# A Fourier mixing layer and a mixture of experts: stage four in even and odd products on quarters of the array

## The chip, the cores and the metric

The kernel runs on one core of one Trainium2 chip. The metric is the device time of one execution in microseconds, as the median of several runs. A core has TensorE (matrix products out of SBUF into PSUM, which has eight banks of 2 KB per partition), VectorE, ScalarE and GpSimd (called DVE, ACT and POOL in the profile), and SyncE (SP), which here issues most of the transfers. Each engine works through its own list of instructions in order and waits on semaphores where one needs another's result.

## What is computed

The first half multiplies each batch of 2496 tokens by 256 features with a filter in the frequency domain, along the tokens. The second sends each token to the one of 8 experts with the largest logit, applies two matrix products with a ReLU between them, and scales by the gate.

```python
# 8 batches, S = 2496, D = 256; all fp32
X = np.fft.rfft(x, axis=1)
y = np.fft.irfft(X * (filt_r + 1j * filt_i)[None], n=S, axis=1)
x = y.reshape(19968, 256)
logits = x @ w_gate                      # (256, 8)
e = np.argmax(logits, axis=1)
gate = softmax(logits)[range(N), e]
out[t] = gate[t] * (np.maximum(x[t] @ w1[e], 0) @ w2[e])   # w1 (8,256,1024), w2 (8,1024,256)
```

## The kernel before

The transform of length 2496 is split as 39 times 64 (the two have no common factor, so tokens and frequencies are only renumbered, and nothing is multiplied in between). A real transform of length 39 has 20 frequencies, each with a real and an imaginary part. So a batch goes through four stages, each a product with a fixed table: stage one (`stage_a`, table `ta`) takes 39 tokens to 20 complex frequencies, stage two (`stage_b`, `tb`) does the complex transform of length 64 and multiplies by the filter, stage three (`stage_c`, `tc`) goes back over the 64, and stage four (`stage_d`, table `td`, tile `tds`) takes 20 complex frequencies back to 39 real tokens. Three groups of 39 tokens stand side by side, so stage four multiplies 3 x 40 = 120 rows onto 3 x 39 = 117 outputs (padded to 128). A batch has 22 such columns of 256 features (the last has only one group, 40 rows). They come in chunks of four, `CH`: five of four columns and one of two. A product takes two columns, which fill one bank of 512 fp32. So a chunk of four is two products, each followed by a copy out of the bank into `yo` (`evac`, which picks VectorE or ScalarE by which the planner thinks is free first). In a chunk of two each column has a product of its own, of 120 and of 40 rows.

Between stages one and two and between three and four the data go through DRAM (`zd`, `ud`), since the partition axis changes: `stage_c` stores four frequencies of all 64 x 2 rows with one transfer of 4 KB runs per partition (`by_part`), and `load_u` reads whole columns of 120 rows (`columns`) into `fin`. Batch 0 is turned on the chip instead (`first_a`, `turn_z`, `first_c`, `turn_u`).

After stage four, `turn_y` transposes `yo` in blocks of 32 on VectorE (from batch 3 on), `block_logits` multiplies by the gate weights on four column quarters of the array (tile `lt`), `block_back` turns the logits back, and `route` finds expert, gate and the row of each token in a list by expert, writes token number and gate behind its features in `yo`, and scatters each column with one indirect transfer of GpSimd into `rows`. `tile_map` and `rows_in` then take tiles of 512, 256 or 128 rows of one expert from there. `first_products` and `second_products` are the two streams of the experts' products. Tiles of 512 rows use seven quarter products in place of eight (`hidden_by_quarters`, and after the last batch also `result_by_quarters`, the sums of whose weights are made on GpSimd into `tsum`); the plain way is `hidden` and `result`.

The order of the work is written out by a planner in the kernel itself. `Order` keeps a clock for each engine and an estimate for each instruction. `slot(k)` lists the steps of stage two and three of batch k, stage one of batch k + 1 and stage four of batch k - 1, each with a place between 0 and 1, what must be loaded, its TensorE time, a category (steps of one category stay in order) and what it needs. The main loop takes, each time, the first step or expert product whose needs are met by the planned clocks, `share()` of expert time for each unit of transform time. PSUM has seven banks for products; `bank()` takes the one that comes free first by the plan. `more_loads` issues loads ahead into seven `fin` tiles, `flush` sends stores when their data are due. All transfers but scatters are on SP's queue, in the order in which the planner wrote them. Every instruction is issued through one helper, line 246, so the profile's rows are told apart by the tiles' names and not by lines.

Of the kernel before, what the change touches and what calls it, by code (L numbers as in the profile page):

```python
# [19 lines left out]
P = 128  # L20
# [14 lines left out]
TK = NB * NS  # L35
DH = D // P
# [4 lines left out]
NJ = D // CT  # L41

# [13 lines left out]
def dft_tables():  # L56

    w = 2.0 * np.pi
    q = np.arange(N1)
    t = np.arange(N2)

    ta = np.zeros((NB, N1, NB, NS))
    td = np.zeros((NB, NS, NB, N1))
    for f in range(NF):
        ang = w * ((q * f) % N1) / N1
        for j in range(NB):  # L70
            ta[j, :, j, f] = np.cos(ang)
            td[j, f, j] = (2.0 if f else 1.0) / S * np.cos(ang)
            if f:
                ta[j, :, j, NF + f] = -np.sin(ang)
                td[j, NF + f, j] = -2.0 / S * np.sin(ang)

    ang = w * ((t[:, None] * t[None, :]) % N2) / N2
    c, sn = np.cos(ang), np.sin(ang)
    tb = np.block([[c, -sn], [sn, c]]).reshape(2, N2, P).transpose(1, 0, 2).reshape(P, P)
    tc = np.block([[c, sn], [-sn, c]]).reshape(P, 2, N2).transpose(0, 2, 1).reshape(P, P)  # L80

    ids = np.zeros((NB, N1, NG))
    valid = np.zeros((NB, N1, NG))
    for j in range(NB):
        for i in range(len(range(j, N2, NB))):
            ids[j, :, i] = token(q, NB * i + j)
            valid[j, :, i] = 1.0

    by_block = np.zeros((4, CT, NG + 2))
    by_block.reshape(P, NG + 2)[:TP, :NG] = valid.reshape(TP, NG)  # L90
    by_block = by_block.reshape(4, CT, -1, 4).transpose(3, 1, 2, 0).reshape(P, -1)

    sg = np.where(coefficients() <= S // 2, 1.0, -1.0)

    return {
        "ta": ta.reshape(TP, TK),
        "tb": tb,
        "tc": tc,
        "td": np.pad(td.reshape(TK, TP), ((0, 0), (0, P - TP))),
        "sg": np.concatenate([sg[:, :NF // 2], sg[:, NF // 2:]]),  # L100
        "ids": ids.reshape(TP, NG),
        "valid": np.concatenate([np.pad(valid.reshape(TP, NG), ((0, P - TP), (0, 0))), by_block], axis=1),
    }


def lay_x(x):

    out = np.zeros((x.shape[0], P, NG, D), x.dtype)
    q = np.arange(N1)
    for j in range(NB):  # L110
        for i in range(len(range(j, N2, NB))):
            out[:, j * N1:(j + 1) * N1, i] = x[:, token(q, NB * i + j)]
    return out
# [11 lines left out]
class Order:  # L125
# [53 lines left out]
    def count(self, engine, op, args, named):  # L179
# [21 lines left out]
        if op.endswith("dma_start"):  # L201
            busy = 1.03 if engine == "gpsimd" else 0.4
            if engine == "sync":
                start = max(start, self.lands[-8])
            self.t[engine] = start + busy
            took = self.transfer(out, named["in_"])
            self.t["transfers"] = max(self.t["transfers"], start + busy) + took
            end, tail = self.t["transfers"], self.LOAD
            if engine == "sync":
                self.lands = self.lands[-7:] + [end + tail]  # L210
        else:
            if out is None:
                took = 0.8 if engine == "sync" else 0.02
            elif engine == "tensor":
                if start > self.busy + 1.2:
                    self.slow = start + 3.4
                rows = out.ap[0][1]
                took = max(0.1, 0.00085 * n) if op == "transpose" else max(0.216, 0.00169 * n) if rows > 32 else 0.00045 * n
                took *= 2.0 if start < self.slow else 1.0
                tail = 0.25  # L220
            elif engine == "vector":
                took = 0.15 + n / 960
            elif engine == "scalar":
                took = 0.16 + n / 1200
            else:
                took = 0.2 + n / 480
            end = self.t[engine] = start + took
            if engine == "tensor":
                self.busy = end
# [21 lines left out]
class Slots:  # L251
# [3 lines left out]
    def freed(self, name, tag):  # L255
# [3 lines left out]
        if tag in self.live and name in self.live[tag]():  # L259
            return 1e9  # L260
# [33 lines left out]
def kernel(  # L294
# [12 lines left out]
    ids: bass.AP,  # L307
    valid: bass.AP,
# [25 lines left out]
    TR = E * TE  # L334

    dram = open_pool(ctx, name="dram", bufs=1, space=DRAM)
    zd = [dram.tile([N2, NS, D], F32, tag=f"z{b % 2}", name="zd") for b in range(B)]
    ud = [dram.tile([N2, NS, D], F32, tag=f"u{b % 2}", name="ud") for b in range(B)]
# [3 lines left out]
    rowsd = dram.tile([TR, DR], F32, tag="rows", name="rows")  # L342
# [17 lines left out]

    tas = cst.tile([TP, TK], F32, name="tas")
    tbs = cst.tile([P, P], F32, name="tbs")
    tcs = cst.tile([P, P], F32, name="tcs")
    tds = cst.tile([TK, P], F32, name="tds")
# [15 lines left out]
    ids0 = cst.tile([TP, NG], F32, name="ids0")  # L380
    vld = cst.tile([P, 2 * NG + 2], F32, name="vld")
# [12 lines left out]
    ps.live["bank"] = lambda: ()  # L394
# [25 lines left out]
    def load_filters(c):  # L420
        f0, n = FH[c]
        if c == 0:
            nc.sync.dma_start(out=tbs, in_=tb)
            nc.sync.dma_start(out=sgs, in_=sg)
# [10 lines left out]
        if c == 0:  # L435
            nc.sync.dma_start(out=tcs, in_=tcm)

    def load_rest():
        nc.sync.dma_start(out=tds, in_=td)
# [33 lines left out]
    def columns(ap, i0, n):  # L473

        rows = ap.rearrange("t s d -> (t s) d")
        m = min(n, NG - 1 - i0)
        yield TK, slice(0, m), rows[i0 * TK:(i0 + m) * TK, :].rearrange("(i p) d -> p i d", p=TK)
        if m < n:
            yield NS, slice(m, n), rows[(NG - 1) * TK:, :].rearrange("(i p) d -> p i d", p=NS)
# [23 lines left out]
    def by_part(ap):  # L503

        return ap.rearrange("t (c f) d -> (t c) f d", c=2)

# [8 lines left out]
    def load_z(b, c):  # L515
        f0, n = FH[c]
        zi = fin(("z", b, c))
        nc.sync.dma_start(out=zi[:, :n], in_=by_part(zd[b])[:, f0:f0 + n, :])

    def load_u(b, c):  # L520
        i0, n = CH[c]
        ui = fin(("u", b, c))
        for r, m, v in columns(ud[b], i0, n):
# [5 lines left out]

    def stage_a(b, c):  # L530
        i0, n = CH[c]
        xt = ins.pop(("x", b, c))
        zo = sb.tile([TK, 4, D], F32, tag="st", name="zo", bufs=4)
        for j in range(0, n, 2):
            p = bank()
            mm(p[:TK, :], lhsT=tas, rhs=xt[:TP, j:j + 2, :], start=True, stop=True)
            evac(zo[:, j:j + 2, :], p[:TK, :].rearrange("p (t d) -> p t d", t=2), 512)
        for r, m, v in columns(zd[b], i0, n):
# [4 lines left out]
    def stage_b(b, f):  # L543
# [6 lines left out]
        mm(p, lhsT=tbs, rhs=zi[:, j:j + 2, :], start=True, stop=True)  # L550
# [14 lines left out]
    def stage_c(b, f):  # L565
# [4 lines left out]
        uo = outs["u", b]  # L570
        p = bank()
        mm(p, lhsT=tcs, rhs=ys, start=True, stop=True)
        evac(uo[:, j:j + 2, :], p.rearrange("p (i d) -> p i d", i=2), 512)
        if j == 2:
            f0 = f - 2
            move(by_part(ud[b])[:, f0:f0 + 4, :], uo)
# [3 lines left out]
    def stage_d(b, c):  # L580
# [7 lines left out]
        yo = outs["o", b, c] = sb.tile([P, 4, DR], F32, tag="y", name="yo", bufs=YB)  # L588
        for j in range(0, n, 2):
            p = bank()  # L590
            if i0 + j + 2 < NG:
                mm(p, lhsT=tds, rhs=ui[:TK, j:j + 2, :], start=True, stop=True)
# [6 lines left out]


# [12 lines left out]
    def first_a(c):  # L613
        i0, n = CH[c]
        xt = ins.pop(("x", 0, c))
        for j in range(0, n, 2):
            p = bank()[:, :4 * TK]
            for h in range(DH):
                for i in range(2):
                    mm(p[:, (2 * h + i) * TK:(2 * h + i + 1) * TK], lhsT=xt[:TP, j + i, h * P:(h + 1) * P], rhs=tas,  # L620
# [21 lines left out]
    def first_c(f):  # L642
        ys = outs.pop(("y", 0, f))
        p = bank().rearrange("p (h i t c) -> p h i t c", h=DH, c=2, i=2)
        for i in range(2):
            for h in range(DH):
                mm(p[:, h, i].rearrange("p t c -> p (t c)"), lhsT=ys[:, i, h * P:(h + 1) * P],
                   rhs=tcs, start=True, stop=True)
# [90 lines left out]
    def route(b, c0, c1):  # L739
# [63 lines left out]
        if by_blocks(b):  # L803
# [13 lines left out]
            nc.vector.tensor_copy(row.rearrange("p (c g) -> p g c", g=4), pr[:, :, 0])  # L817
# [5 lines left out]
        for i, yo in enumerate(yos):  # L823
            n = min(4, w - 4 * i)
            sh8 = (TP, n, 8)
            nc.gpsimd.tensor_scalar(
                yo.bitcast(I32)[:TP, :n, D:D + 8], in0=ids0[:, t0 + 4 * i:t0 + 4 * i + n, None].to_broadcast(sh8),
# [3 lines left out]
        for i in range(w):  # L831
            m = N1 if t0 + i == NG - 1 else TP
# [116 lines left out]
    def rows_in(i):  # L949
# [4 lines left out]
        ng = gis[i] = pools["moe"].tile([P, 4, DR - D], F32, tag="ng", name="ng", bufs=8)  # L954
# [262 lines left out]
    def slot(k):  # L1217
# [12 lines left out]
        elif k < B:  # L1230
            for f in range(0, NF + 4, 2):
                at = f / (NF + 4)
                if f < NF:
                    steps.append((at, lambda f=f: stage_b(k, f), ("z", k, f // 4) if f % 4 == 0 else None, 0.85, "b", lambda f=f: count("y") < 4 and [ins["z", k, f // 4]]))
                if f >= 4:
                    steps.append((at + 0.01, lambda f=f: stage_c(k, f - 4), None, 0.85, "c", lambda f=f: [outs["y", k, f - 4], 0.0 if f % 4 else sb.free("st") - 0.9]))
        if k + 1 < B:
            for c in range(nch):
                steps.append(((0.25 if k == 0 else 0.0) + 0.7 * c / nch, lambda c=c: stage_a(k + 1, c), ("x", k + 1, c), 0.43 * CH[c][1], "a", lambda c=c: [ins["x", k + 1, c], sb.free("st") - 0.9]))
        if k > 0:  # L1240
            for c in range(nch + 3):
# [3 lines left out]
                if c < nch:  # L1245
                    steps.append((at, lambda c=c: stage_d(k - 1, c), ("u", k - 1, c) if k > 1 else "y", 0.43 * CH[c][1], "d",
                                  lambda c=c: [ins["u", k - 1, c] if k > 1 else outs["ui", c], sb.free("y") - 0.9]))
                if by_blocks(k - 1):
                    if 1 <= c <= nch:
                        steps.append((at + 0.03, lambda c=c: turn_y(k - 1, c - 1), None, 0.0, "d", lambda c=c: len(yts) < 2 and [outs["o", k - 1, c - 1]]))  # L1250
# [174 lines left out]
    def second_products():  # L1425

        for i in range(NT - RARE):
            if late and i < LARGE:
# [37 lines left out]
    with tc.manual_schedule(engines=None):  # L1466
        warm()
        nc.sync.dma_start(out=tas, in_=ta)
# [5 lines left out]
        def wait_of(f):  # L1474
# [11 lines left out]
            banks = ps.free("bank") if f[3] < 0.9 else max(ps.free("bank"), ps.free("bank", 1) - 0.85)  # L1486
# [15 lines left out]
        while fs or any(heads):  # L1502
# [7 lines left out]
            choice[0 if credit > 0.0 or not fs else 1:0] = products  # L1510
# [64 lines left out]
```

## Time and profile before

| | |
|---|---|
| median of 5 runs | 1477.38 us (1475.93 to 1479.08) |
| the profiled execution | 1477.88 us, of which its span 1476.2 us |
| mean granted clock of TensorE | 0.994 |
| TensorE busy | 1440.2 us, 98% of the span |
| VectorE, ScalarE, GpSimd busy | 848.1, 480.7, 821.5 us |
| stage four's products (`bank<-fin,tds`, batches 1 to 7) | 168 records, 77.8 us busy |
| bytes moved | 278.19 MB, 188 GB/s in the mean |

How to read the lines further down: a group is `line engine operation out<-in shapes xcount | busy us, mean ns of one | idle time of the engine before it, and what ended it`. PE is TensorE's matmul, PEld its weight load. [...] Records overlap, so the time that a group takes is read from the start of the group to the start of the next and not from its length. In a timeline line the first two numbers are start and length in us. In a table by stretch, each engine's busy us stand with its number of records, then TensorE's granted clock, the busy share of the DMA engines and GB/s. `fin`, `uo`, `yo`, `lt`, `ys`, `hT`, `w1t`, `w2t` are tiles of the kernel, `bank` is PSUM.

### The profile page before, as it was taken

The numbers are of one execution on the slowest core, as the hardware profiler recorded it, in microseconds if no ns is written. First come the engines' busy times: TensorE is split into PE (matmuls) and PEld (weight loads), VectorE is DVE, ScalarE is ACT, GpSimd is POOL, SyncE is SP. The second block draws the span as 40 slices with busy tenths as digits, with TensorE's granted clock in tenths as the row PEclk, the third lists the DMA queues.
The fourth block names the chain that finished last, engine by engine and source line by source line (L and its number), as shares of the span: only waits on it lengthen the run. The fifth ranks groups of instructions, "written<-read, shape, count | busy, mean of one in ns | idle before, by whom it ended". The sixth has DMA issues, their size and how long they took to land.

```text
span 1476.2 us, 25693 instructions
## 1 busy us (share of the span) xinstructions
PE 1440.2 (98%) x7828; PEld 1148.1 (78%) x7828; DVE 848.1 (57%) x1819; ACT 480.7 (33%) x1004; POOL 821.5 (56%) x1213
## 2 busy tenths in 40 slices
PE   8998998999999999999999999999999999999998
PEld 6643555777677777886777778879999999999997
DVE  4666669336765675566666465666878775431110
ACT  4553452333323333232223332222232322223332
POOL 3434355625545644745565657758989888831111
PEclk9998999999999999999999999999999999999999
DMA  9759798896885485556544634566665424456661
GB/s 249 249 186 322 272 306 266 246 272 219 300 217 171 145 285 155 144 153 233 130 135 140 199 110 136 159 172 188 169 178 161 142 82 139 134 190 176 174 190 43
DMA packets 216383, 278.19 MB, mean 188 GB/s; under 512 B 124131, under 2 KB 163708, under 8 KB 216245
## 3 DMA queue, kind: packets, MB, share of 16 engines
q1 hardware_dynamic: 197125, 233.19, 53.9%
q0 software_dynamic: 19120, 43.33, 8.4%
q8 instruction: 66, 1.08, 0.3%
q14 instruction: 72, 0.59, 0.1%
HBM read 196.45 MB, written 80.64 MB: 188 GB/s over the span
## 4 chain that ended last, share of the span: by engine, by line
PE 85%; DVE 6%; DMA 4%; issue 3%; SPq 1%; ACT 0%; POOL 0%; DVEq 0%; POOLq 0%; ACTq 0%
PE bank L246 84%; DMA fin<-in_x_dram 2%; DVE yw L246 2%; PE lt L246 1%; DVE ys L246 1%; DVE hT L246 1%; DMA fin<-ud 1%; SPq L246 1%; DMA fin<-zd 1%; DMA zd<-zo 1%; POOL out_dram L246 0%; DMA w1t<-in_moe_w_dram 0%; DVE take L246 0%; DMA xg<-rows 0%; DVE oh L246 0%
## 5 line engine op out<-in xcount | busy, mean ns | idle before, releaser
L246 DVE TENSOR_TENSOR hT<-bank,hT 128x512 f32<-128x512 f32 (+1 forms) x504 | 301.2, 626 | 172.6 <-PE bank L246 105.2
L246 PE MATMUL bank<-w2t,hT 128*128 128x256 f32 (+1 forms) x1984 | 388.6, 350 | 1.6 <-DVE hT L246 1.6
L246 PEld LDWEIGHTS bank<-w2t,hT 128*128 128x128 f32 x1984 | 334.6, 190 | 49.8 <-issue 9.9
L246 PE MATMUL bank<-xT,w1t 128*128 128x256 f32 (+1 forms) x1728 | 315.6, 329 | 0.0
L246 POOL DMA_INDIRECT out_dram<-ys,ng x161 | 160.1, 994 | 254.1 <-ACT ys L246 132.9
L246 PEld LDWEIGHTS bank<-xT,w1t 128*128 128x128 f32 x1728 | 265.3, 191 | 32.8 <-issue 9.4
L246 ACT ACTIVATE hT<-hT 128x1024 f32<-128x1024 f32 (+1 forms) x144 | 134.9, 959 | 392.3 <-DVE hT L246 392.2
L246 POOL DMA_INDIRECT rows<-yo,row x176 | 181.6, 1032 | 70.7 <-POOL yo L246 54.2
L246 ACT ACTIVATE ys<-bank,ng 128x256 f32<-128x256 f32 x102 | 48.4, 474 | 294.1 <-PE bank L246 266.0
L246 PE MATMUL bank<-sums,wsum 128*128 128x256 f32 (+1 forms) x576 | 135.7, 358 | 1.5 <-DVE hT L246 1.5
L246 PE MATMUL bank<-w2s,hT 128*128 x592 | 132.7, 379 | 0.0
L246 PEld LDWEIGHTS bank<-w2s,hT 128*128 128x128 f32 x592 | 110.3, 190 | 13.9
L246 POOL TENSOR_TENSOR wsum<-w1t 128x256 f32<-128x256 f32 x72 | 57.4, 798 | 108.2 <-PE bank L246 91.1
L246 PEld LDWEIGHTS bank<-sums,wsum 128*128 128x128 f32 x576 | 100.3, 190 | 21.6 <-issue 11.2
L246 DVE STREAM_TRANSPOSE xT<-xg 128x512 f32<-128x512 f32 (+2 forms) x126 | 57.4, 494 | 58.6 <-PE bank L246 43.5
L246 DVE TENSOR_TENSOR ys<-bank,ht 128x512 f32<-128x512 f32 x80 | 54.9, 686 | 47.1 <-PE bank L246 41.7
L246 PE MATMUL bank<-fin,tas 117*120 117x512 f32 x154 | 74.9, 604 | 6.8 <-DMA fin<-in_x_dram 6.7
L246 PE MATMUL bank<-fin,tds 120*128 120x512 f32 (+1 forms) x168 | 77.8, 584 | 3.4 <-DMA fin<-ud 2.8
L246 PE MATMUL bank<-ys,tcs 128*128 128x512 f32 x140 | 74.7, 621 | 6.4 <-DVE yw L246 4.5
L246 PE MATMUL bank<-fin,tbs 128*128 128x512 f32 x140 | 72.7, 607 | 3.2 <-DMA fin<-zd 3.2
L246 ACT ACTIVATE hT<-bank 128x128 f32<-128x128 f32 (+1 forms) x191 | 57.5, 303 | 52.9 <-PE bank L246 50.2
L246 PE MATMUL bank<-xT,wsum 128*128 128x256 f32 (+1 forms) x288 | 68.7, 361 | 0.9 <-DVE yw L246 0.9
(171 smaller groups left out, 1782.3 us busy)
## 6 DMA issues: line engine op xcount, KB each, us to landing
w1t<-in_moe_w_dram SPq DMA_DIRECT2D x126, 512.0 KB
w2t<-in_moe_w_dram SPq DMA_DIRECT2D x68, 512.0 KB
fin<-in_x_dram SPq DMA_DIRECT2D x39, 512.0 KB
fin<-zd SPq DMA_DIRECT2D x35, 512.0 KB
ud<-uo SPq DMA_DIRECT2D x35, 512.0 KB
fin<-ud SPq DMA_DIRECT2D x35, 512.0 KB
zd<-zo SPq DMA_DIRECT2D x35, 480.0 KB
xg<-rows SPq DMA_DIRECT2D x112, 128.0 KB
```

What stands on the lines that cost most here:

```text
L246: return real(*args, **named)
```

## The change

From batch 3 on (`BD = 3`) stage four is done in another way. A real transform back from 20 frequencies is, for token q, the sum of a part that is even in q (the real rows, cosines) and one that is odd (the imaginary rows, sines); token 39 - q is the difference of the two. So `stage_d` takes the 60 real rows (3 groups of 20) to the even part of tokens 0 to 19 of the three groups, 60 outputs, and the 60 imaginary rows to the odd part. The real rows stand in partitions 0 to 59, the imaginary ones in 64 to 123. For a chunk of four columns there are four products of 60 rows by 64 columns: even and odd, for the first two and for the last two columns of the chunk, each on one quarter of the array (rows by part, columns by half of the chunk), into two banks: one with all even parts, one with all odd parts, 512 per partition. `evac` copies the odd bank into the second half of `yo`; the even bank stays, and a new step, `fold_y`, writes sum and difference with two VectorE operations, which read the bank and `yo`. A chunk of two columns does the same with 256.

With it go:

- `tc` is loaded a second time for batches from 3 on with its outputs reordered, so that real and imaginary rows of three groups follow each other, and `td` gets a second table; `load_table` puts both into the tile of the first.
- `ud` has columns of 128 rows. The stores of `stage_c` go as 126 partitions and 2 partitions, two transfers in place of one. Two more transfers per batch, ahead of them, fill the unused rows with numbers (of the filter) so that what is loaded is defined. A load reads 128 rows of all columns of a chunk in one transfer.
- Tokens stand elsewhere in `yo`, so `route` has new token numbers (`lids`), 124 rows for each column, and unused places, which are sent to 320 spare rows per batch behind the list; the row number is the larger of the found one and the spare one.
- The planner: products of 64 outputs have times of their own, a bank that waits for `fold_y` is not free, steps of `stage_a` and `stage_d` categories want two free banks, steps without TensorE time want none, `fold_y` is a category of its own, and an expert product is put behind the first step that is not such a fold.
- `ng` has seven buffers instead of eight. The first late tile goes by `result_by_quarters` only where its sums have been begun.
- The same for stage one (`fold_x`, `BA`) is in the code, but with `BA = 8` no batch uses it.

```diff
+TH = NB * NF                 # 60
+YR = 64 + TH
+BA, BD = 8, 3
+NW = P * NG - S              # 320
...
-    zd = [dram.tile([N2, NS, D], F32, tag=f"z{b % 2}", name="zd") for b in range(B)]
-    ud = [dram.tile([N2, NS, D], F32, tag=f"u{b % 2}", name="ud") for b in range(B)]
+    zd = [dram.tile([NG * P, D], F32, tag=f"z{b % 2}", name="zd") for b in range(B)]
+    ud = [dram.tile([NG * P, D], F32, tag=f"u{b % 2}", name="ud") for b in range(B)]
...
+    def load_table(name, of, k):
+        tables[name] = cst.tile([P, P], F32, tag=name, name=name)
+        nc.sync.dma_start(out=tables[name], in_=of[k])
...
-    ps.live["bank"] = lambda: ()
+    ps.live["bank"] = lambda: {p.name for key, p in outs.items() if key[0] == "odd"}
...
+    def by_part(rows, tile, quarters, f0, n):
+        if not quarters:
+            yield tile[:, :n], rows[:N2 * NS].rearrange("(t c f) d -> (t c) f d", c=2, f=NF)[:, f0:f0 + n, :]
+            return
+        m = 2 * (NG - 1)
+        for lo, hi, r in ((0, m * NB, NB), (m * NB, P, 1)):
+            at = rows[lo // NB * 64 + f0, :]
+            to = tile[lo:hi, :n]
+            dims = [[64 * D, (hi - lo) // r]] + ([[NF * D, r]] if r > 1 else []) + [[1, n * D]]
+            yield bass.AP(to.tensor, to.offset, [list(to.ap[0]), [1, n * D]]), bass.AP(at.tensor, at.offset, dims)
...
     def stage_c(b, f):
...
+        if b >= BD and f == 0:
+            at = ud[b][TH, :]
+            nc.sync.dma_start(out=bass.AP(at.tensor, at.offset, [[64 * D, 2 * NG - 2], [1, 4 * D]]), in_=ht[:2 * NG - 2, :4, :].rearrange("p f d -> p (f d)"))
+            nc.sync.dma_start(out=ud[b][(NG - 1) * P:, :], in_=ht[:, 0, :])
...
-            move(by_part(ud[b])[:, f0:f0 + 4, :], uo)
+            for of, v in by_part(ud[b], uo, b >= BD, f0, 4):
+                move(v, of)
...
     def stage_d(b, c):
...
+        if b >= BD:
+            m = n // 2
+            both = [bank() for _ in range(2)]
+            for h in range(2):
+                for part in range(2):
+                    k = slice(64 * part, 64 * part + TH)
+                    mm(both[part][64 * h:64 * h + 64, :m * D].rearrange("p (i d) -> p i d", i=m), lhsT=tds[k, :64],
+                       rhs=ui[k, h * m:(h + 1) * m, :], start=True, stop=True)
+            evac(yo[:, m:n, :D], both[1][:, :m * D].rearrange("p (i d) -> p i d", i=m), m * D)
+            outs["odd", b, c] = both[0]
+            return
...
+    def fold_y(b, c):
+        m = CH[c][1] // 2
+        even = outs.pop(("odd", b, c))[:, :m * D].rearrange("p (i d) -> p i d", i=m)
+        yo = outs["o", b, c]
+        nc.vector.tensor_tensor(yo[:, :m, :D], even, yo[:, m:2 * m, :D], op=ALU.add)
+        nc.vector.tensor_tensor(yo[:, m:2 * m, :D], even, yo[:, m:2 * m, :D], op=ALU.subtract)
...
-            nc.vector.tensor_copy(row.rearrange("p (c g) -> p g c", g=4), pr[:, :, 0])
+            nc.vector.scalar_tensor_tensor(
+                out=row.rearrange("p (c g) -> p g c", g=4),
+                in0=lids[:, NG + t0:NG + t0 + wide].rearrange("p (c g) -> p g c", g=4), scalar=float(b * NW),
+                in1=pr[:, :, 0], op0=ALU.add, op1=ALU.max)
...
-            m = N1 if t0 + i == NG - 1 else TP
+            m = YR if b >= BD else N1 if t0 + i == NG - 1 else TP
...
-        ng = gis[i] = pools["moe"].tile([P, 4, DR - D], F32, tag="ng", name="ng", bufs=8)
+        ng = gis[i] = pools["moe"].tile([P, 4, DR - D], F32, tag="ng", name="ng", bufs=7)
...
+        for name, of, when, where in (("ta", ta, BA - 1, "a"), ("tb", tb, BA, "b"), ("tc", tcm, BD, "c"), ("td", td, BD + 1, "d")):
+            if k == when:
+                steps.append((-1.0, lambda name=name, of=of: load_table(name, of, 1), None, 0.0, where))
+        if k == BD:
+            steps.append((0.5, lambda: nc.sync.dma_start(out=lids, in_=late_ids), None, 0.0, "x"))
...
+                if c < nch and k > BD:
+                    steps.append((at + 0.001, lambda c=c: fold_y(k - 1, c), None, 0.0, "y", lambda c=c: [outs["odd", k - 1, c], outs["o", k - 1, c]]))
...
-            if late and i < LARGE:
+            if late and i < LARGE and (wide or i in made):
...
-            banks = ps.free("bank") if f[3] < 0.9 else max(ps.free("bank"), ps.free("bank", 1) - 0.85)
+            banks = 0.0 if not f[3] else ps.free("bank") if f[3] < 0.9 and f[4] not in "ad" else max(ps.free("bank"), ps.free("bank", 1) - 0.85)
...
-            choice[0 if credit > 0.0 or not fs else 1:0] = products
+            head = next((n for n, c in enumerate(choice) if c[0][4] not in ("x", "y")), 0) + 1
+            choice[0 if credit > 0.0 or not fs else head:0] = products
```

## The prediction, made before the change was run

> **What bounds the kernel now.** I read the page first: share of TensorE, its slices, and the chain that ended last.
>
> ```profile
> PE 1440.2 (98%) x7828; PEld 1148.1 (78%) x7828; DVE 848.1 (57%) x1819; ACT 480.7 (33%) x1004; POOL 821.5 (56%) x1213
> ...
> PEclk9998999999999999999999999999999999999999
> ...
> PE 85%; DVE 6%; DMA 4%; issue 3%; SPq 1%; ACT 0%; POOL 0%; DVEq 0%; POOLq 0%; ACTq 0%
> ```
>
> TensorE runs through at full clock, and the chain is its own work. But 98% is an average, so I asked next in which stretch the change lies. Stage four of batch 3 starts at 288.4 us and that of batch 7 ends at about 883; so I took the busy times up to 300 us, those from 300 to 900, and TensorE's waits in the second stretch.
>
> ```profile
> 0.00:300.00 300.00, 278.52 (x1204) 172.98 (x1205) 185.34 (x459) 130.35 (x279) 138.94 (x224) 0.97 0.83 264
> ```
> ```profile
> 300.00:900.00 600.00, 595.11 (x2961) 449.28 (x2961) 368.03 (x773) 184.56 (x364) 329.59 (x518) 1.00 0.62 185
> ```
> ```profile
> PE bank L246 <- DVE ys L246: 1.1, 1, 1.1
> PE lt L246 <- DVE yt L246: 1.0, 1, 1.0
> PE bank L246 <- DVE yw L246: 0.9, 1, 0.9
> PE bank L246 <- DVE ls L246: 0.8, 1, 0.8
> PE bank L246 <- DVE oe L246: 0.5, 1, 0.5
> PE bank L246 <- ACT hT L246: 0.4, 1, 0.4
> ```
>
> The columns after the length are busy us of PE, PEld, DVE, ACT, POOL, then clock, DMA share and GB/s. Before 300 us TensorE is idle for 21.5 us, behind transfers above all; from 300 to 900 it is idle for 4.9 us, never behind a transfer, and VectorE has 232 us to spare. A microsecond of TensorE's work saved after 300 us is thus a microsecond of the span, as long as no other engine takes the lead.
>
> **What the change removes: TensorE's time in stage four.** The timeline of TensorE has the price of a chunk, as the distance from its first start to the next group's start.
>
> ```profile
> 324.83 1.88 PE L246 MATMUL bank<-fin,tds 120*128 120x512 f32 x4
> 326.55 1.03 PE L246 MATMUL bank<-xT,w1t 128*128 128x256 f32 x4
> 327.51 0.65 PE L246 MATMUL lt<-yt,wb 128*32 128x128 f32 x16
> 328.08 2.21 PE L246 MATMUL bank<-w2t,hT 128*128 128x256 f32 x9
> ```
> ```profile
> 348.37 1.22 PE L246 MATMUL bank<-fin,tds 120*128 120x256 f32 x4
> 349.52 1.78 PE L246 MATMUL bank<-w2t,hT 128*128 128x256 f32 x7
> ```
> ```profile
> 1007.27 1.95 PE L246 MATMUL bank<-w2t,hT 128*128 128x128 f32 x16
> 1009.05 1.25 PE L246 MATMUL bank<-xT,w1t 128*128 128x256 f32 x5
> ```
>
> Each fp32 product leaves two records. A chunk of four columns is two products, four records: 326.55 - 324.83 = 1.72 us, 0.43 a record. The last chunk of a batch (two columns, as 120 and 40 rows) takes 349.52 - 348.37 = 1.15. Its four records of 256 columns would be 0.86 by half of 0.43 each; 0.29 is lost where the 40-row product stands.
>
> New: four products of 60 rows onto 64 outputs, each in a quarter of the array of its own. Eight records of 512 columns, which are 8 x 0.43 = 3.44 us if they run one after another, 4 x 0.43 if two at a time, 2 x 0.43 = 0.86 if four at a time. The trace shows quarters by columns: the logits' group lt has 16 records of 128 columns on 32 outputs in 328.08 - 327.51 = 0.57, while 16 full-width ones of the same length take 1009.05 - 1007.27 = 1.78, 0.111 each. 0.57 is four waves of 0.111 and 0.13 over; another 0.09 is lost ahead of it (326.55 to 327.51 is 0.96, the four records of 256 columns are 0.87). So four streams at a time work in column quarters, at 0.22 a visit. Halves by rows no group here shows. I take four at a time, because the four quarters read and write as the lt group does but for the row split, and between 0.22 (lt) and 0.29 (the 40-row product) I take 0.25 a visit: 0.86 + 0.25 = 1.11 for a large chunk, 0.43 + 0.25 = 0.68 for the small. Saved: 25 x (1.72 - 1.11) = 15.3 and 5 x (1.15 - 0.68) = 2.4, together **17.7 us**. With 0.22 and 0.29 it would be 18.6 and 16.5.
>
> [...]
>
> **What it adds on VectorE and ScalarE.** Before, a chunk has two evictions, on ScalarE for the most part. After, one eviction and two sums that read a bank and `yo`.
>
> ```profile
> L246 DVE TENSOR_TENSOR ys<-bank,ht 128x512 f32<-128x512 f32 x80 | 54.9, 686 | 47.1 <-PE bank L246 41.7 <-ACT zo L246 5.1
> ...
> L246 DVE TENSOR_TENSOR low<-bank,three 128x256 f32<-128x256 f32 x18 | 7.6, 425 | 15.7 <-PE bank L246 15.7
> ```
> ```profile
> L246 ACT COPY yo<-bank 128x512 f32<-128x512 f32 x82 | 47.8, 586 | 42.4 <-PE bank L246 39.9 <-issue 1.2 <-DMA rows<-yo,row 0.8
> ```
>
> 25 x 2 x 0.686 + 5 x 2 x 0.425 = 38.6 us more on VectorE, and some 25 x 0.59 = 15 less on ScalarE. VectorE goes from 368 to about 407 in a stretch that shrinks to 583: 61% becomes 70%. The sums wait for the four products and the copy (0.59 of ScalarE), and behind them stand the hT sums, stage two's products and the transposes of yt; for those TensorE waits through its banks. The even bank is held some 0.6 + 1.4 us longer, one of seven. Cover: between two steps of the transforms lie the experts' products, which need no new bank content from stage four. VectorE released 4.3 us of TensorE's idle time above; bounds are 0 (all stays covered) and 12, a third of the added work being exposed. I take 2.5, a little over half as much again, since most of the time VectorE still has 30% free.
>
> [...]
>
> **What it moves or adds on the queues.** SP: a second transfer with each of 25 stores of `uo`, two fillers for each of five batches, `lids`, two tables, less five loads: 33 issues; of the kind `ud<-uo` the trace has a median of 0.33 us, 11 us over 600. The two tables wait on SP for the last stage-three product of batch 2 and the last stage-four product of batch 2; behind them stand loads of `fin`, w1t and w2t, for which the products wait. The store over the filled last column waits for the filler, which was sent some steps earlier. SP already stands 227.4 us behind TensorE's banks in this stretch without one wait of TensorE for a transfer; I count 0, at most 3. POOL: scatters of 124 rows for 117, and for 39 in the last column. Medians are 1.006 us and 0.912 at the least; as (1.006 - 0.912) / 78 rows = 1.2 ns a row, 110 of them cost 1.4 us, on an engine with 270 us free: 0. The mask on `row` replaces a copy of 128x8 by one operation of that size; seven `ng` for eight frees a tile later, for which nothing of TensorE waits now: 0 both.
>
> The planner's own changes reorder the list: the shorter steps of stages one and four (small chunks, turns) now want two free banks instead of one, in all batches, and steps without TensorE time want none. It changes when loads are issued before 300 us, where 21.5 us idle may become less or more: -4 to +4, I take 0. At the end a result tile goes by quarters of the experts' sums only if its sums were begun: the first such sum starts at 998.0 and the last plain group runs till 1001.2, so it is close. Lost, one tile goes from 7 x 1.78 = 12.5 to 64 x 0.217 = 13.9: 0 to +1.4, I take 0.3.
>
> **Sum.** The profiled execution took 1477.88 us (span 1476.2 and 1.7 around it), 0.5 above the median of 1477.38. 1477.9 - 17.7 + 2.5 + 0.3 = 1463.0, by the median's level 1462.5. I say **1463**.
>
> **Rivals.** *Given back on VectorE*: the sums push hT sums back and banks run out; with 8 us exposed instead of 2.5 it is 1468 to 1475, at the middle 1470. For it: TensorE's idle time after 300 us is VectorE's nearly alone. Against: 30% left free. *Row halves don't overlap*: two quarters at a time, so a chunk is 1.72 + 0.25 = 1.97 and a small one 0.86 + 0.25 = 1.11; 25 x 0.25 - 5 x 0.04 = +6, with VectorE's 2.5 it is **1486**, slower. It decides from 3.4 waves a chunk on ((1.72 - 0.25) / 0.43). For it: no row-split group in this trace, and a 40-row product that loses 0.29. Against: the lt group's four streams. One at a time it would be 3.69 a chunk, 1477 + 49 + 5 = 1531. *The order slips*: the new list costs 10 to 20 us by transfers before 300 us or a starved expert stream: 1475 to 1483. For it: 83% DMA share there; against: those steps' needs hardly change. *The change doesn't do what it says* would be quarters that leave TensorE's distance per chunk at 1.7; that is the second rival's border.
>
> **Numbers.** Forecast 0.63 (its own range 1458 to 1468), given back 0.17, row halves 0.11, the order 0.09. A change within 0.2% (1474.4 to 1480.3) can't be told from none. Faster: 0.63 + 0.16 = 0.79; same: 0.01 + 0.05 = 0.06; slower: 0.11 + 0.04 = 0.15. The range 1458 to 1477 leaves out 0.15 and a little of the forecast's lower end.
>
> **What would show it.** A large chunk's distance of 1.0 to 1.2 us, with eight records in two waves 0.43 apart: the saving stands; 1.9 or more: it falls. VectorE 400 to 410 us busy in the stretch of stage four and TensorE's waits for it under 8 us: its price stands. TensorE idle before 300 us near 21, and nine tiles by quarters (288 records tsum with hsum): the order stands. The first wrong sign would be a long row of waits for a bank behind `yo`.

## The result, and the profile after

The changed kernel takes 1480.27 us (median of 38 runs, 1473.58 to 1486.7) against 1476.79 for the kernel before in the same series (64 runs, 1469.78 to 1482.63). The ratio is 1.0024, 95% interval [1.0015, 1.0033]: 3.5 us slower, where 14 us faster was forecast. The profiled execution took 1484.01 us with a span of 1482.3, 6.1 above the span before.

TensorE's timeline has the new chunks, a large one and the small one of a batch.

```profile
386.62 1.09 PE L296 MATMUL bank<-fin,td 60*64 60x512 f32 x8
387.63 1.55 PE L296 MATMUL bank<-fin,ta 117*120 117x512 f32 x3
```
```profile
474.94 0.66 PE L296 MATMUL bank<-fin,td 60*64 60x256 f32 x8
475.53 1.13 PE L296 MATMUL bank<-sums,wsum 128*128 128x256 f32 x4
```

The distances are 387.63 - 386.62 = 1.01 us and 0.59, where 1.72 and 1.15 stood before; nearly every other chunk of batches 3 to 7 has the same. So the four quarters do run four at a time, and TensorE gives up 25 x 0.71 + 5 x 0.56 = 20.6 us. The change does what it says, and more than the 17.7 us counted on. The gain is lost elsewhere. Busy time by stretch and TensorE's waits after 300 us:

```profile
0.00:300.00 300.00, 274.30 (x1207) 166.72 (x1208) 183.06 (x442) 128.58 (x277) 135.63 (x220) 0.97 0.86 262
```
```profile
300.00:900.00 600.00, 582.56 (x3014) 435.55 (x3013) 393.01 (x837) 169.31 (x337) 352.68 (x510) 0.99 0.66 190
```
```profile
PE bank L296 <- DVE yw L296: 6.1, 3, 2.7
PE bank L296 <- DMA w2t<-in_moe_w_dram: 4.1, 2, 3.0
PE bank L296 <- DMA fin<-ud: 2.0, 2, 1.5
PE bank L296 <- DVE hT L296: 1.9, 2, 1.0
PE bank L296 <- DVE yo L296: 1.1, 1, 1.1
```

TensorE is now idle for 17.4 us between 300 and 900 (4.9 before) and for 25.7 before 300 (21.5). VectorE is busy for 393 us of 600, 66% on the mean. What the mean hides is seen in one place, in TensorE's and VectorE's timelines and in the busy times of the same 8 us:

```profile
482.12 1.03 PE L296 MATMUL bank<-xT,w1t 128*128 128x256 f32 x4
484.25 0.26 PE L296 MATMUL bank<-rx,sel 128*32 128x16 f32 x8 [1.10 <-DVE yo L296]
486.34 1.89 PE L296 MATMUL bank<-ys,tc 128*128 128x512 f32 x2 [1.83 <-DVE yw L296]
```
```profile
483.10 0.22 DVE L296 TENSOR_TENSOR rx<-rs,msk 128x64 f32<-128x64 f32 x1
483.24 0.17 DVE L296 COPY cnt<-tot 128x8 f32<-128x8 f32 x1
483.32 0.88 DVE L296 TENSOR_TENSOR yo<-bank,yo 128x256 f32<-128x256 f32 x2
484.11 0.68 DVE L296 TENSOR_TENSOR ys<-bank,ht 128x512 f32<-128x512 f32 x1
484.81 0.69 DVE L296 SCALAR_TENSOR_TENSOR yw<-bank,ht 64x512 f32<-64x512 f32 x1
485.51 0.68 DVE L296 TENSOR_TENSOR yw<-bank,ht 64x512 f32<-64x512 f32 x1
```
```profile
482.00:490.00 8.00, 5.07 (x19) 2.35 (x18) 7.31 (x16) 1.53 (x2) 2.38 (x4) 0.79 0.01 2
486.50:489.90 3.40, 3.40 (x5) 1.24 (x5) 2.93 (x5) 1.53 (x2) 1.60 (x3) 0.50 0.01 2
```

The product rx,sel of `route` has its input at 483.32, but it goes only at 484.25, when the sums of `fold_y` (`yo<-bank,yo`) have emptied a bank; the next product stands till the third operation of stage two has read another. TensorE has no record between 484.51 and 486.34: what comes next in its list waits too. VectorE is busy for 7.31 of these 8 us, and the only wait listed for it there is one of 0.39 us behind 488.7. After these two waits TensorE's clock is 0.50 for 3.4 us, from 486.5 on. The same stands from 353.4, 527.5 and 708.4: the last two also follow waits at a product rx,sel (2.97 and 4.14 us in three waits each), but the first follows a wait for a transfer.

```profile
352.65 1.75 PE L296 MATMUL bank<-w2t,hT 128*128 128x256 f32 x5 [3.02 <-DMA w2t<-in_moe_w_dram]
```
```profile
353.40:356.80 3.40, 3.40 (x10) 2.68 (x9) 0.00 (x0) 0.00 (x0) 3.01 (x6) 0.50 0.71 263
```

Two records ys,tc take 1.89 us from 486.34 where two from 701.39 take 1.02. Taken as 3.4 us at a clock of 0.50, each stretch costs 1.7 us, an estimate; before has none of it between 250 and 1470 us. What starts a stretch is not shown: the waits ahead of the four are 3.02, 2.93, 2.97 and 4.14 us in all, the longest by itself 3.02.

The account of the two profiled executions: -20.6 for stage four; +12.5 idle from 300 to 900 us; 4 x 1.7 = +6.8 at half clock there; +4.2 idle before 300, and at most +1.7 at half clock there (six stretches of 3.4 us against five); +1.4 for one result tile that no longer goes by quarters (the products of tsum with hsum are 256 records, 288 before); -3.1 for two waits of before, at 981 and 985 us, that are gone. That is +2.9 of the 6.1. Where the other 3 us lie these views don't show.

Two rows had not been foreseen: scatters take longer, and SP waits longer for them.

```profile
L296 POOL DMA_INDIRECT rows<-yo,row x176 | 217.6, 1236 | 75.6 <-POOL yo L296 57.7
```
```profile
SPq L296 <- DMA rows<-yo,row: 58.5, 8, 12.3
```

They were 181.6 us and 1032 ns, and SP's wait between 300 and 900 us was 20.0 us.

### The profile page after: what moved, and what is told of

It is laid out like the page before. It is cut to its first block, busy times and chain, and to the rows that moved or that the text cites. A ratio compares the mean times of both kernels' runs of the same rounds, so it can differ in the third digit from the quotient of the medians.

```text
span 1482.3 us, 25899 instructions
## 1 busy us (share of the span) xinstructions
PE 1432.5 (97%) x7900; PEld 1134.1 (77%) x7900; DVE 866.5 (58%) x1870; ACT 463.4 (31%) x976; POOL 848.9 (57%) x1211
## 2 busy tenths in 40 slices
DMA packets 227476, 281.87 MB, mean 190 GB/s; under 512 B 133926, under 2 KB 173866, under 8 KB 227338
## 5 line engine op out<-in xcount | busy, mean ns | idle before, releaser
L296 PE MATMUL bank<-w2t,hT 128*128 128x256 f32 (+1 forms) x1984 | 402.3, 357 | 5.4 <-DMA w2t<-in_moe_w_dram 4.1
L296 PEld LDWEIGHTS bank<-w2t,hT 128*128 128x128 f32 x1984 | 343.3, 193 | 62.2 <-issue 13.8
L296 POOL DMA_INDIRECT rows<-yo,row x176 | 217.6, 1236 | 75.6 <-POOL yo L296 57.7
L296 PE MATMUL bank<-fin,tb 128*128 128x512 f32 x140 | 74.6, 622 | 10.2 <-DMA fin<-zd 9.2
L296 PE MATMUL bank<-fin,ta 117*120 117x512 f32 x154 | 75.4, 608 | 5.7 <-DMA fin<-in_x_dram 5.0
L296 PE MATMUL bank<-ys,tc 128*128 128x512 f32 x140 | 73.7, 613 | 7.2 <-DVE ys L296 4.2
L296 PE MATMUL bank<-sums,w1t 128*128 128x256 f32 (+1 forms) x288 | 67.3, 356 | 0.2 <-ACT hT L296 0.2
```

The costliest lines, as they stand in the source:

```text
L296: return real(*args, **named)
```

## The experiments

In them theory B is that VectorE's added work is what costs; theory A puts it on the scatters, and theory C on the order that the planner writes. Each ratio is to the kernel before on the same chip; the differences between experiments are quotients of these ratios, times 1477.

**e1: scatters of 128 rows.** Order and work else as in the changed kernel.

```diff
-            m, at = (TP, ids0) if b < BD else (YR, lids[:YR])
+            m, at = (TP, ids0) if b < BD else (P, lids)
...
-            m = YR if b >= BD else N1 if t0 + i == NG - 1 else TP
+            m = P if b >= BD else N1 if t0 + i == NG - 1 else TP
```

> The changed kernel, only that the scatters of batches 3 to 7 send all 128 rows of a column (the four unused rows of each half go to spare rows too) instead of 124. The list of instructions on every engine stays the same. Theory A (a 124-row scatter is slow, the rows come late, SP stands before the rows' loads and weights behind them come late): a scatter goes back from 1.34 us to about 1.0, SP's wait for the rows from 58.5 us between 300 and 900 us to 20 to 30, TensorE no longer waits 3 us for w2t near 350, and the time is 4 to 9 us under the changed kernel's 1480. Theory B (the sums of stage four pile up on VectorE and banks run out) and theory C (the planner's new rules made a worse order): scatters may get shorter, the time stays within 2 us of 1480.

Ratio 1.0001 [0.9986, 1.0017], about 3.4 us less than the changed kernel. By the two intervals it can be 1 to 6 us, between A's 4 to 9 and the 2 that B and C allow. The group of scatters and SP's wait:

```profile
L296 POOL DMA_INDIRECT rows<-yo,row x176 | 178.9, 1017 | 69.8 <-POOL yo L296 30.9
```
```profile
SPq L296 <- DMA rows<-yo,row: 33.1, 6, 7.5
```

GpSimd gets its 39 us back, and TensorE's wait for w2t falls from 4.1 to 0.8 us; but its waits for VectorE stay to the digit (6.1 behind yw, 1.9 behind hT, 1.1 behind yo), and the clock from 300 to 900 us is 0.99 as in the changed kernel. A holds, for a small part.

**e2: the first sum of `fold_y` written three times.**

```diff
         nc.vector.tensor_tensor(yo[:, :m, :D], even, yo[:, m:2 * m, :D], op=ALU.add)
+        for _ in range(2):
+            tc.nc.vector.tensor_tensor(yo[:, :m, :D], even, yo[:, m:2 * m, :D], op=ALU.add)
```

> The changed kernel with the sum in fold_y written three times (same inputs, same result), so two more VectorE operations of 0.69 us for each chunk, 38 us more in all, and the even bank held 1.4 us longer; the planner doesn't count them, so the order is that of the changed kernel. Theory B: as the first pair of operations is what cost the gain, a second pair costs as much or more: 10 to 20 us over 1480, with waits of TensorE for VectorE growing from 9 us to 20 or more. Theories A and C: VectorE has a third of its time free, so 0 to 4 us more.

Ratio 1.0082 [1.0058, 1.0105]: 8.6 us more than the changed kernel for 38 us more of VectorE. The listed waits for VectorE rise to 15.8 us, not to 20, and the time by a little less than B had it. It is twice what A and C allow.

**e3: the new rules alone, on the kernel before.** The edit is two of the last three parts of the change's diff (`banks`; the condition on `made`) and seven `ng`; the new place of expert products in the choice is not in it. One of the lines:

```diff
-            banks = ps.free("bank") if f[3] < 0.9 else max(ps.free("bank"), ps.free("bank", 1) - 0.85)
+            banks = 0.0 if not f[3] else ps.free("bank") if f[3] < 0.9 and f[4] not in "ad" else max(ps.free("bank"), ps.free("bank", 1) - 0.85)
```

> The kernel before with the planner's rules of the change alone (two free banks for steps of stages one and four, none for steps without TensorE time, the condition on the first late result tile, seven ng buffers); stage four itself is the old one. Theory C: the order is what costs, so 5 to 15 us over before's 1477. Theories A and B: within 3 us of before, at most the 1.4 us of the one result tile.

Ratio 0.9973 [0.9957, 0.9990]: 4 us *faster* than before, even with eight tiles by quarters instead of nine. These rules are a gain, so the rest of the change, stage four's new form with its scatters and transfers, costs 7.5 us from here to the changed kernel. From 300 to 900 us:

```profile
300.00:900.00 600.00, 594.19 (x2946) 449.13 (x2938) 368.08 (x778) 184.04 (x363) 329.58 (x521) 1.00 0.61 184
```

**e4: the changed kernel with the old rules.** The same lines turned back, and the place of expert products in the choice.

> The changed kernel with the old planner rules (one free bank for short steps, old place of expert products in the choice, old condition on the first late result tile); ng stays at seven, the quarters and the scatters stay. Theory C: the gain comes back, 1465 to 1472. Theories A and B: within 4 us of 1480, less the 1.4 us of a ninth result tile by quarters.

Ratio 1.0071 [1.0048, 1.0093], 7 us over the changed kernel. Every theory missed this, and C falls: the rules as a whole help the new form. But 5.0 us of it is a single wait near 1021 us, when the first late tile goes by quarters before its sums are made:

```profile
PE bank L296 <- POOL tsum L296: 5.0, 1, 5.0
```

The changed kernel has no such wait; it's the condition on `made` that avoids it. What the other rules are worth in the new form, 3 us or so after that and the ninth tile's 1.4, is within the noise of the two intervals.

**e5: `route` asks for a bank** (on e1).

```diff
-            while t["tensor"] < nc.ready(rx) + 1.0:
+            while t["tensor"] < max(nc.ready(rx) + 1.0, ps.free("bank") + 0.5):
```

and the same with `oe` ahead of the ranks.

> The changed kernel with scatters of 128 rows, and route lets its products (ranks, and the turn of the found rows) go only when a bank is free by the planner's clock half a microsecond later at most. If TensorE's waits at the products rx,sel (9 us with what follows them, and three stretches of half clock) come only from where route puts them, they go and the time falls by 8 to 12 us against e1 (ratio to before 0.992 to 0.995). If VectorE is simply behind there, the wait moves to the next product that needs a bank, and the time stays within 3 us of e1.

Ratio 0.9934 [0.9910, 0.9958], 9.9 us less than e1. TensorE's waits behind yw fall from 6.1 to 1.0 us. The order is another, and ten result tiles go by quarters in place of eight, which is some 2.8 us of it. The three waits behind yw in the changed kernel all come at or just behind a product rx,sel of `route`, so the loss shows where a small product takes a bank without asking; that this and not the rest of the new order brings the gain is not shown apart. VectorE is busy for 410 of the 600 us here, 68%, and TensorE is idle for 8.7 only.

**e6: stage two's last sum on GpSimd, order unchanged** (on e1).

```diff
+        elif b >= BD:
+            nc.count("vector", "tensor_tensor", (ys, ys, yw), {"op": ALU.add})
+            tc.nc.gpsimd.tensor_tensor(ys, ys, yw, op=ALU.add)
```

> As e1 (128-row scatters), with the last sum of stage two (ys + yw) of batches 3 to 7 on GpSimd instead of VectorE, 50 operations of 0.73 us off VectorE and of about 1.3 us onto GpSimd; the order is that of the changed kernel on every other engine. VectorE then has as much to do as before the change. If the sums of stage four cost by filling VectorE, TensorE's waits for VectorE fall from 9 us to under 3 and the time by 6 to 12 us against e1. If not, or if GpSimd becomes late instead, it stays within 3 us or gets slower.

Ratio 0.9941 [0.9918, 0.9965], 8.9 us less than e1 for 36 us of operations off VectorE. It is e2 with the sign turned. The waits don't fall under 3 us: 3.8 behind yw stay, and 1.1 behind GpSimd's new sum come. TensorE is idle for 10.4 us, against 14.4 in e1:

```profile
300.00:900.00 600.00, 589.65 (x3096) 442.26 (x3095) 381.88 (x821) 172.63 (x343) 370.99 (x563) 1.00 0.64 194
```

**e7 and e8: the same, known to the planner**, in the new form (on e1) and in the old (on e3).

```diff
-        if b == 0 or b < 3 and not sides:
+        if b == 0 or b < 3 and not sides or b >= BD:
```

> As e6, and the planner knows of it and writes its order for it. If VectorE set the pace of the written order too, TensorE's gain of 20 us in stage four comes out in full: 18 to 26 us under before (ratio 0.982 to 0.988). If VectorE has nothing to do with it, as e1: ratio 0.998 to 1.002.

> e3 (the old stage four with the new planner rules) with the same sum of batches 3 to 7 on GpSimd. If VectorE is what stage four's new form lacks, the old form gains little by it, 0 to 5 us against e3 (ratio 0.994 to 0.998), and the distance from here to e7 is the worth of the new stage four with VectorE relieved, 14 us or more. If the relief itself is worth as much in both forms, e8 is as far below e3 as e7 is below e1.

e7: 0.9887 [0.9861, 0.9912], 16.8 us less than e1 and 17 less than before, short of the 18 to 26 expected. e8: 0.9995 [0.9978, 1.0012], no gain over e3 (3 us more, but the intervals overlap). Both have ten result tiles by quarters where e1 and e3 have eight, some 2.8 us of each step. Busy times from 300 to 900 us, e7 and then e8:

```profile
300.00:900.00 600.00, 599.60 (x3178) 455.18 (x3177) 388.01 (x849) 179.28 (x366) 393.59 (x585) 1.00 0.65 197
```
```profile
300.00:900.00 600.00, 598.71 (x3006) 460.27 (x3005) 349.54 (x769) 185.96 (x381) 376.74 (x561) 1.00 0.61 186
```

Both leave TensorE next to nothing to wait for (0.4 and 1.3 us idle). In the old form there was little to win in this stretch (5.8 us idle in e3), and e8 loses before 300 us (26.7 idle against 22.2, at a clock of 0.95 against 0.98); in the new form the relief lets most of stage four's gain out: e7 is 16 us under e8, against 4 us *over* it for the same pair without relief (e1 and e3). e7's VectorE is busy for 388 us, hardly less than the changed kernel's 393, but in the same 600 us it does the work of more steps (3178 TensorE records against 3014).

**e9: fillers and second tables on ScalarE's queue** (on e1).

```diff
-            nc.sync.dma_start(out=ud[b][(NG - 1) * P:, :], in_=ht[:, 0, :])
+            nc.count("sync", "dma_start", (), dict(out=ud[b][(NG - 1) * P:, :], in_=ht[:, 0, :]))
+            tc.nc.scalar.dma_start(out=ud[b][(NG - 1) * P:, :], in_=ht[:, 0, :])
...
```

and the same for the other filler and the tables.

> e1 with the two fillers per batch and the second tables issued on ScalarE's queue instead of SP's; the planner counts them as before, so the order is that of e1. If SP's issue time before the loads of batch 3 makes TensorE's long wait near 256 us and some of the later ones, the time falls by 2 to 6 us against e1 and TensorE's idle time before 283 us from 28 us to about 25. If the transfers themselves or the order make it, it stays within 2 us, or rises where ScalarE stands behind a table's wait.

Ratio 1.0071 [1.0048, 1.0094], 10 us more than e1. One wait of TensorE for `fin<-zd` before 300 us is now 12.5 us; the longest was 4.4 in e1 and 6.4 in the changed kernel. ScalarE has its longest wait for TensorE's bank (15.5 us) in this run, but whether the tables' loads held back its evictions is not shown. What the transfers of batch 3 cost before 300 us stays open.

**e10: e7 and e5 together.**

> e7 (128-row scatters, stage two's last sum on GpSimd and planned so) with route asking for a bank as in e5. If the products of route have banks in e7 anyway, the same within 3 us as e7 (ratio to before 0.987 to 0.990); if some of its waits are still theirs, 3 to 6 us less.

Ratio 0.9882 [0.9855, 0.9909], as e7. In e7 the one wait listed for TensorE from 297 to 905 us is 0.4 us, for `lt`: route's products have their bank there. e7 and e10 are the fastest versions found.

**e12 and e13: VectorE's load in the old form.** On e3, stage four's evictions of batches 3 to 7 a second time by VectorE (e12), or stage two's first product twice (e13), both uncounted by the planner.

```diff
+            if b >= 3:
+                tc.nc.vector.tensor_copy(yo[:, j:j + 2, :D], p.rearrange("p (i d) -> p i d", i=2))
```
```diff
+        if b >= 3:
+            tc.nc.vector.tensor_mul(ys, z2, ht[:, f:f + 2, :])
```

> e3 (old stage four, new rules) with each eviction of stage four of batches 3 to 7 written a second time by VectorE, 55 copies of 0.68 us that the planner doesn't count: VectorE gets the load that the change gives it, TensorE has its old work and order. If VectorE had the 30% free that the forecast counted on, the time rises by 0 to 3 us over e3. If VectorE's load alone makes the loss, whatever TensorE does, it rises by 8 us or more, as with the tripled sums. Between them, 3 to 8, old stage four's 1.72 us of TensorE without VectorE's work was the room that took the load, and the change took that room away as it added the load.

> e3 (old stage four, new rules) with stage two's first product of batches 3 to 7 written twice, 50 operations of 0.69 us, 34 us more on VectorE that the planner doesn't count and that wait for nothing new. The copies of e12 stood 26 us behind ScalarE's evictions, so its loss mixes load and waits. If the load alone costs, this is 6 to 14 us over e3 (ratio to before 1.001 to 1.007); if it was the waits, 0 to 4 over e3.

e12: 1.0085 [1.0063, 1.0107], 16.6 us over e3; in its trace VectorE also stands 26.2 us behind ScalarE's evictions, so load and wait are mixed. e13: 1.0044 [1.0027, 1.0061], 10.5 us over e3 for 34 us of load alone:

```profile
300.00:900.00 600.00, 589.88 (x2895) 444.94 (x2894) 386.11 (x798) 181.40 (x358) 323.06 (x511) 0.99 0.60 183
```

TensorE, with its old work and its old order, is idle for 10.1 us here where e3 has 5.8, at a VectorE that is 64% busy. So the old order had no room for such work either, and a microsecond of it cost 0.31, no less than in the new form (0.23 in e2).

## Why the prediction was wrong, point by point

**What bounds the kernel** was right for TensorE, but the conclusion was not: that VectorE "has 232 us to spare" between 300 and 900 us. Free time on the mean is not free time where it is needed. Of the signs named, a chunk's distance came (1.0 us); VectorE's 393 us, the 9.1 us of listed waits for it, the 25.7 us idle before 300 and the eight tiles by quarters all missed. The sign to come first, a long row of waits behind `yo`, hardly came (1.1 us): the sums delay what stands behind them on VectorE, so the waits are behind yw (6.1).

**Stage four on TensorE** was right, and the quarters by rows work: 20.6 us for 17.7. The rival that row halves don't overlap falls (its one-at-a-time figure, 1531, is 1 too high by its own terms).

**The failed step is the price of VectorE's added work**, 2.5 us of 38.6 (the trace has 38.5) with bounds of 0 and 12, taken "since most of the time VectorE still has 30% free". By fixed order it measures 8.6 us for the second such load (e2), 8.9 for taking as much away (e6) and 10.5 for 34 us in the old form (e13): a quarter to a third of the load shows, near the upper bound and far from the middle. The planner's order for a relieved VectorE brings 8 more (e6 to e7), 2.8 of them by the two result tiles. What I had named as cover, the experts' products between two steps of the transforms, covers less than I took: they need banks and VectorE's sums themselves (`hT<-bank,hT`, 1.9 us of TensorE's waits). The old chunk may also have been a rest for VectorE, 1.72 us of TensorE with the copies on ScalarE where the new one is 1.01 us with 1.4 of VectorE; that isn't shown, and e13, whose load cost no less with the old chunks, speaks against it. The kernel gives its products seven banks, and from 300 to 900 us TensorE stood 9.1 us behind VectorE. The waits are joined by the half clock, 4 x 1.7 us by the estimate above, which no term held and which the measured prices include.

**The queues** were counted as nothing. The scatters are wrong by their row: 124 rows were priced by the slope between columns of 39 and of 117 rows, 1.2 ns a row, and cost 0.33 us more each; e1 puts that at some 3 us. SP's second tables and fillers may hold a part of the 4.2 us idle before 300; e9 didn't settle it.

**The planner's rules** were taken at 0 between -4 and +4: -4 by e3, without the new place of expert products. The lost result tile came, at its upper bound, and e4 shows that it avoided a wait of 5 us.

**The rivals.** "Given back on VectorE" had the mechanism and, with 8 us exposed, nearly the price at fixed order; its 1470 lacked the other terms. "The order slips" gave the right time by luck: the rules help, and what was lost before 300 us is the smaller part. Put together, the runs give -20.6 for stage four, -4 for the rules and the tile (e3), +3.4 for scatters (e1), +9 for VectorE at fixed order (e2, e6), +5 for the order that follows from VectorE's clock (e6 to e7 without the tiles) and +5.9 lost before 300 us: -1.3, where +3.5 was measured. The terms come from different orders, so the sum is rough, and some 5 us stay open.

## What to carry to other kernels

Where an engine in order empties PSUM for TensorE, price work added to it by what stands in the same microseconds and not by its mean share: here VectorE was busy 61 to 66% of the time, and each microsecond added or taken away moved the time by 0.23 to 0.31, while another order (e5) ran faster at 68%. A run that adds a known load at fixed order measures this price before the change is made. Moving as much off that engine, with an order written for it and e1's scatters (e7), made a loss of 0.2% a gain of 1.1%. A small product that takes a bank without asking can stop everything behind it, as at 484 us (1.10 us at the product itself, 1.83 behind it).

## What the runs showed of the hardware that was not expected

- An indirect scatter of 124 rows of 1088 bytes takes 1.34 us on GpSimd (the median), one of 117 rows 1.01; with 128 rows (e1) the mean of all scatters is back at 1.017. The trace with 124 rows has 133,926 packets under 512 bytes, against 124,131 before and 123,366 in e1. Why 124 rows differ was not tried.
- Four fp32 products of 60 rows on 64 columns, on the four quarters of the array, take 1.01 us with 512 columns and 0.59 with 256, from their first start to the start of the next group.
- In the changed kernel's four cases from 300 to 900 us, waits of TensorE of 2.9 to 4.1 us in all, none longer than 3.02 by itself, were followed by one stretch of 3.4 us at half clock.
